# Norms ahead of the K phase, a later weight load and an earlier first gate/up block in a two-layer attention and gated-MLP kernel

## The chip, the cores and the metric

The kernel runs on one core of a Trainium2 chip. The metric is the device time of one execution in microseconds (us). Executions of the kernel before agree within 0.4%. "Faster" or "slower" needs 2%. A profile also shows TensorE's granted clock, as a share of full speed; in every profile here it is either 1.0 or 0.5 ("half clock"), and a mean between them is a mixture.

## The reference, cut to what matters

```python
x = A_x                                          # 2048 tokens x 576, bf16
x = x + A(layernorm(x), wqkv, w_phi, wo)         # attention
x = x + B(layernorm(x), w_gate, w_up, w_down)    # (x@w_gate * x@w_up) @ w_down, 4608 wide
x = x + A(layernorm(x), wqkv, w_phi, wo)         # the same again: "layer 2"
x = x + B(layernorm(x), w_gate, w_up, w_down)

def A(x, wqkv, w_phi, wo):      # linear attention, 32 heads of 18
    q, k, v = heads(x @ wqkv)
    phi_q = concat(softmax(q @ w_phi), softmax(-(q @ w_phi)))    # per head
    phi_k = concat(softmax(k @ w_phi), softmax(-(k @ w_phi)))
    kv, z = phi_k^T @ v, sum_s phi_k             # over ALL tokens
    return (phi_q @ kv) / (phi_q @ z + 1e-6) @ wo
```

The sum over all tokens is a barrier: no attention output exists before the last K tile is done. The MLP (gate, up, down) has none.

## The kernel before

The tokens form 16 tiles of 128 and 8 blocks of two tiles (a pair). Python "threads" describe the work (a pair's layer norm, a tile's K softmax, a tile's attention output, a block of gate/up, its down), and a list scheduler puts their instructions into one fixed order per engine before anything runs. At each step it takes the request that could start first; the priority decides between equals and who gets a shared buffer first, and some priorities have a head start, the "bias", in ns:

```python
key = (est - self.bias.get(int(th.prio), 0.0), -th.prio)      # smallest key is issued next
self.NPS, self.NSM, self.NVX, self.NET, ... = 2, 4, 2, 3, ... # buffers shared by the threads
self.qlead, self.pace, self.bias = 3, (4, 3), {10: 300.0}
```

So the order that runs on the chip is the one that the scheduler's own durations gave.

```python
def t_layer1(self):                          # K phase of layer 1, cut
    for b in range(NB):
        yield ("wait", ("ld", "x", b))
        yield ("go", s.t_ln(b, ("xT", 1, b)), 6, ...)              # norm of a pair, DMA transposes
        if b >= 1:
            yield ("wait", ("xT", 1, b - 1))
            for j in range(2):
                yield ("go", s.t_ain(1, 2 * b - 2 + j), 6 + ..., ...)   # K softmax, V, K^T V
    yield ("go", s.t_barrier(1), 9, "bar1")  # masks K^T V into BD
    yield ("go", s.t_q(1), 5, "q1")          # starts the outputs, pair after pair:
#   for b in range(NB):
#       if b >= s.pace[L - 1]: wait for the down of block b - pace
#       for j in range(2): yield ("go", s.t_aout(L, 2 * b + j), 7 + ..., ...)

def pol1(b):                                 # what block b of gate/up waits for besides its own norm
    if b + 1 < NB:
        ev += [("x1", 1, 2 * b + 2), ("x1", 1, 2 * b + 3)]         # outputs of the NEXT pair
```

A tile's output thread (`t_aout`) first makes the "front" (Q projection and softmax, transposes), which doesn't need BD, then waits for BD and makes the rest. `x1` is a tile's state after the attention output has been added.

Of the kernel before, what the change touches and what calls it, by code (L numbers as in the profile page):

```python
# [229 lines left out]
class _Thread:  # L230
    __slots__ = ("gen", "prio", "req", "name", "deps_cache", "est", "t_ready", "seq")
# [14 lines left out]
class Sched:  # L246

    def __init__(self, tracker):
        self.tr = tracker
        self.free_at = {e: 0.0 for e in ENGINES}  # L250
        self.busy = {e: 0.0 for e in ENGINES}
        self.threads = []
        self.pools = {}
        self.events = set()
        self.ev_time = {}
        self.dma_free = {e: 0.0 for e in ENGINES}
        self.dma_bw = 280.0
        self.dma_lat = 2000.0
        self.log = []
        self.bias = {}  # L260
        self.pe_mode = 0
        self.pe_switch = 100.0
        self.lock = None

# [56 lines left out]
    def run(self):  # L321
        tr = self.tr
        while True:
            progressed = False
            again = True
            while again:
                again = False
                for th in list(self.threads):
                    while th.req is not None and th.req[0] not in ("ops", "dma", "acq", "acqn"):
# [26 lines left out]
                        elif kind == "unlock":  # L356
                            assert self.lock is th
                            self.lock = None
                            self._advance(th, None)
                        elif kind == "delay":  # L360
# [22 lines left out]
            for th in self.threads:  # L383
                r = th.req
                if r[0] == "ops":
# [20 lines left out]
            r = th.req  # L406
# [46 lines left out]
T0 = [0, TW, 2 * TW, 3 * TW, D - TW]  # L453
# [22 lines left out]

class K:
    def __init__(self, nc, A_x, A_wqkv, A_w_phi, A_wo, B_w_gate, B_w_up, B_w_down, out):
# [3 lines left out]
        self.NPS, self.NSM, self.NVX, self.NET, self.NXP, self.NWD, self.NG, self.NO = 2, 4, 2, 3, 2, 4, 2, 1  # L482
        self.early = 2
        self.qlead = 3
        self.pace = (4, 3)
        self.bias = {10: 300.0}
# [4 lines left out]
    def alloc(self):  # L491
# [8 lines left out]
        self.kvacc = A("kvacc", [TW, NJ, TW + 1], F32)  # L500
# [31 lines left out]
        self.den = A("den", [128, self.NO, NT * HT], F32)  # L532
# [34 lines left out]
    def t_init(self):  # L567
# [30 lines left out]
            Op(100, lambda e: e.memset(s.vx[:, :, :, TW:TW + 1], 1.0), writes=[("vxone",)]),  # L598
# [10 lines left out]
    def t_bdphi(self):  # L609
        s = self  # L610
        yield ("wait", "init")
        yield ("wait", ("ld", "wphi"))
        wb = s.wst[:].unsqueeze(2).to_broadcast([TW, NT, HT, DH])
        mb = s.mask[:].rearrange("p (j d) -> p j d", j=HT).unsqueeze(1).to_broadcast([TW, NT, HT, DH])
        ov = s.BDphi[:].rearrange("p t (j d) -> p t j d", j=HT)
        yield ("ops", "dve", [Op(750, (lambda e: e.tensor_tensor(ov, wb, mb, ALU.mult)),
                                 reads=[("wst",), ("mask",)], writes=[("BDphi",)])])
        yield ("sig", "bdphi")

    def t_load(self):  # L620
# [15 lines left out]
        def rawload(which, kt):  # L636
# [7 lines left out]
                 ((lambda e: e.dma_start(s.wst[:, 4, :], s.A_w_phi[H - HT:H].rearrange("j d f -> (j d) f"))), [("wst",)], TW * DH * 2)]  # L644
# [28 lines left out]
        for i, (emit, writes, nbytes) in enumerate(items):  # L673
            if i % 3 == 0 and 5 + i // 3 < NB:
                yield ("wait", ("xT", 1, 5 + i // 3))
# [4 lines left out]
    def t_fuse(self, which):  # L680
# [7 lines left out]
        for kt in range(5):  # L688
# [6 lines left out]
            for t in range(NT):  # L695
                c0 = off + T0[t]
                ops.append(Op(60, (lambda e, t=t, c0=c0, P=P, kt=kt: e.transpose(P[0:TW, 128 * t:128 * t + 128], s.Wraw[:, kt, c0:c0 + TW], s.ident[:])),
                              reads=[("Wraw", 0, which, kt), ("Wraw", 1), ("ident",)], writes=[("pbd", bank)], excl=[("pb", bank)]))
            yield ("ops", "pe", ops)
            yield ("ops", "act", [Op(700, (lambda e, P=P, wt=wt: e.copy(s.WT[:, wt, :, :], P[0:TW, 0:640].rearrange("p (t n) -> p t n", t=NT))),  # L700
                                     reads=[("pbd", bank)], writes=[("WT", wt)], excl=[("pb", bank)])])
# [3 lines left out]
    def t_fuse2(self, which):  # L705
        s = self
        Wm, km = (s.Wq, "Wq") if which == "q" else (s.Wk, "Wk")
        for kt in range(5):
            yield ("wait", ("wt", which, kt))
            wt = s.wt_of[(which, kt)]  # L710
            for half in range(2):
# [3 lines left out]
                for t in ((0, 1, 2) if half == 0 else (3, 4)):  # L715
                    lo = 0 if t < 4 else 3 * DH
                    n = TW - lo
                    ops.append(Op(d_pe(n) + 25, (lambda e, t=t, c=c, lo=lo, n=n, bank=bank, wt=wt: e.matmul(
                        s.ps[:, bank, c:c + n], s.WT[:, wt, t, :], s.BDphi[:, t, lo:TW], start=True, stop=True)),
# [5 lines left out]
                yield ("ops", "dve", [Op(d_dve(c), (lambda e, bank=bank, c0=c0, c=c, kt=kt, m=m: e.tensor_copy(  # L725
                    Wm[0:m, kt, c0:c0 + c], s.ps[0:m, bank, 0:c])),
                    reads=[("pbd", bank)], writes=[(km,)], excl=[("pb", bank)])])
# [6 lines left out]
    def t_ln(self, b, sig):  # L734
        s = self
        x_sb, xln, st, mv, lnv, rstd, xT = s.x_sb, s.xln, s.st, s.mv, s.lnv, s.rstd, s.xT
        pair = yield ("acq", "xlnp")
        sl = [2 * pair, 2 * pair + 1]
        ss = [2 * b, 2 * b + 1]
        ops = []  # L740
        for j in range(2):
# [5 lines left out]
        for j in range(2):  # L747
# [3 lines left out]
        var2 = mv[:, sl[0]:sl[0] + 2, 1:2].rearrange("p a b -> p (a b)")  # L751
        mean2 = mv[:, sl[0]:sl[0] + 2, 0:1].rearrange("p a b -> p (a b)")
        nm = s.nmean
        yield ("ops", "act", [
            Op(215, (lambda e: e.activation(lnv[:, sl[0]:sl[0] + 2], var2, ACTF.Ln, bias=s.epst[:, 0:1], scale=1.0)),
               reads=[("mv", sl[0]), ("mv", sl[1]), ("epst",)], writes=[("lnv", pair)]),
            Op(160, (lambda e: e.mul(nm[:, sl[0]:sl[0] + 2], mean2, -1.0)),
               reads=[("mv", sl[0]), ("mv", sl[1])], writes=[("nmean", pair)]),
            Op(205, (lambda e: e.activation(rstd[:, sl[0]:sl[0] + 2], lnv[:, sl[0]:sl[0] + 2], ACTF.Exp, scale=-0.5)),  # L759
               reads=[("lnv", pair)], writes=[("rstd", pair)]),  # L760
        ])
        ops = []
        for j in range(2):
            ops.append(Op(800, (lambda e, j=j: e.tensor_scalar(  # L764
                xln[:, sl[j], 0:576], x_sb[:, ss[j], :], nm[:, sl[j]:sl[j] + 1], rstd[:, sl[j]:sl[j] + 1],
                ALU.add, ALU.mult)),
                reads=[("x", ss[j], 0), ("x", ss[j], 1), ("nmean", pair), ("rstd", pair)], writes=[("xln", sl[j])]))
        yield ("ops", "pool", ops)
        yield ("ops", "act", [Op(240, (lambda e: e.copy(xln[:, sl[0]:sl[0] + 2, 576:640], xln[:, sl[0]:sl[0] + 2, 512:576])),
                                 reads=[("xln", sl[0]), ("xln", sl[1])], writes=[("xlnt", pair)])])  # L770
        for j in range(2):
            tok = slice(128 * ss[j], 128 * ss[j] + 128)
            yield ("dma", s.g_xt[sl[j]], (lambda e, j=j, tok=tok: e.dma_start_transpose(xT[:, :, tok], xln[:, sl[j], :])),
                   [("xln", sl[j]), ("xlnt", pair)], [("xT", ss[j])], 128 * 640 * 2, False, True, 1250.0)
        yield ("rel", "xlnp", pair)
        yield ("sig", sig)
# [14 lines left out]
    def softmax_front(self, st_, pz, sm, Wm, km):  # L791
        s = self
        psb, dd, mxmn, ss = s.psb, s.dd, s.mxmn, s.ss
        gots = yield ("acqn", ["pb"], 2)
# [7 lines left out]
        ops = [Op(680, (lambda e: e.tensor_reduce(mxmn[:, pz, 0, :], p3, AX.X, ALU.max)),  # L802
                  reads=[("psb", pz, 0), ("psb", pz, 1)], writes=[("mx", pz)])]
        for h in range(2):
# [7 lines left out]
        yield ("ops", "pool", [Op(1170, (lambda e: e.tensor_tensor(d1, p3, mxb, ALU.subtract)),  # L812
                                  reads=[("psb", pz, 0), ("psb", pz, 1), ("mx", pz)], writes=[("dd", sm, 0)])])
# [31 lines left out]
        for br in range(2):  # L845
            ev = dd[:, sm, br, :].rearrange("p (g e) -> p g e", e=DH)
            rb = ss[:, sm, H * br:H * br + H].unsqueeze(2).to_broadcast([128, H, DH])
            yield ("ops", "pool", [Op(1150, (lambda e, ev=ev, rb=rb: e.tensor_tensor(ev, ev, rb, ALU.mult)),  # L848
                                      reads=s.ddk(sm, br) + [("ss", sm)], writes=s.ddk(sm, br))])

    def t_v(self, L, st_):
# [4 lines left out]
        for h in range(2):  # L856
            (_, bank), = yield ("acqn", ["pb"], 1)
            c0, n = ((0, 3 * TW), (3 * TW, D - 3 * TW))[h]
            yield ("ops", "pe", s.proj(st_, c0, n, s.Wv, "Wv", bank))
            if h == 0:  # L860
                src = s.ps[:, bank, 0:n].rearrange("p (t n) -> p t n", t=3)
                dst = s.vx[:, vxs, 0:3, 0:TW]
# [459 lines left out]
```

## Time and profile before

| | before |
|---|---|
| time, median (lowest to highest of 3 runs) | 1218.46 us (1218.12 to 1219.91) |
| span of the profiled execution | 1212.5 us |
| BD of layer 1 done by VectorE (two clearing memsets of GpSimd follow, until 114.1) | 112.6 us |
| first gate/up matmul, layer 1 / layer 2 | 140.70 / 720.58 us |
| weight load of layer 1's last down matmul ends | 667.63 us |

I cut the span at these events into four stages: prologue, main part of layer 1 (gate/up to the last down), transition, main part of layer 2. The columns are the stretch, its length, then busy time and number of instructions of PE (TensorE's matmuls), PEld (its weight loads), DVE (VectorE), ACT (ScalarE) and POOL (GpSimd), the granted clock, the DMA share and GB/s. Length less PE's busy time is TensorE's idle time.

```profile
0.00:140.70 140.70, 98.64 (x780) 70.59 (x781) 106.15 (x242) 84.11 (x220) 87.00 (x93) 0.85 0.50 142
140.70:667.63 526.93, 519.42 (x7259) 400.77 (x7301) 266.21 (x535) 193.59 (x429) 114.28 (x109) 1.00 0.34 90
667.63:720.58 52.95, 30.19 (x239) 22.17 (x237) 33.97 (x88) 22.46 (x52) 21.83 (x22) 0.81 0.11 27
720.58:1212.50 491.92, 475.73 (x6821) 363.44 (x6856) 191.31 (x380) 142.50 (x276) 50.23 (x48) 1.00 0.35 95
```

TensorE idles 42.1 us of the prologue and 22.8 of the transition. In the main parts PE has fewer records than PEld (42 and 35 fewer), so matmul records are missing and the idle time there, 7.5 and 16.2 us, is too high by several us; I use idle time only for prologue and transition. Two more stretches: two blocks of layer 2, one with a pair of outputs in it and one without.

```profile
8.00:105.00 97.00, 72.34 (x571) 50.07 (x569) 78.92 (x166) 62.59 (x173) 67.26 (x65) 0.88 0.65 187
```

```profile
783.66:846.56 62.90, 61.48 (x880) 47.43 (x886) 27.48 (x57) 20.45 (x40) 8.49 (x8) 1.00 0.32 92
1096.28:1152.37 56.09, 54.58 (x791) 40.40 (x796) 13.99 (x23) 10.85 (x19) 0.00 (x0) 1.00 0.42 110
```

A pair is 90 weight loads (886 less 796) and 6.8 us, 76 ns a load.

### The profile page before, as it was taken

The page shows a single profiled execution, that of the slowest core. Times are in us where ns is not written, and L with a number is a line of the kernel's source. Part 1 is how long each engine was busy: PE and PEld are TensorE (multiplying, and loading weights), DVE is VectorE, ACT ScalarE, POOL GpSimd, SP SyncE. Part 2 cuts the span into 40 slices and gives each one's busy share as a digit, 9 for nine tenths or more (in the row PEclk, how much of TensorE's full clock was granted, in tenths as well). Part 3 has the DMA queues.
Part 4 walks back from the last instruction along what each step waited for, and adds up shares of the span by engine and source line. Part 5 has one row for each costly group of instructions (what it writes and reads, how often), then busy time and mean ns, then how long its engine had stood idle before and what let it go on. Part 6 is the DMA issues. An engine that isn't in the chain of part 4 may idle for free.

```text
span 1212.5 us, 33465 instructions
## 1 busy us (share of the span) xinstructions
PE 1124.0 (93%) x15096; PEld 857.0 (71%) x15172; DVE 597.6 (49%) x1243; ACT 442.7 (37%) x976; POOL 273.3 (23%) x271
## 2 busy tenths in 40 slices
PE   5875899999999999999999579899999999999998
PEld 4554686868777786858585358586868686868584
DVE  7866846373645546343435483235353535353131
ACT  5765543352524334323234353123332323242120
POOL 4785403041322304020203341002020202020000
PEclk8986999999999999999999799999999999999999
DMA  7654007143341506050515100606151424343514
GB/s 175 140 161 170 17 8 183 29 123 78 89 111 51 150 13 173 18 176 13 173 18 147 41 12 13 197 3 171 28 157 43 138 62 128 72 119 81 150 39 147
DMA packets 130336, 115.59 MB, mean 95 GB/s; under 512 B 48914, under 2 KB 129042, under 8 KB 129042
## 3 DMA queue, kind: packets, MB, share of 16 engines
q1 hardware_dynamic: 130194, 113.46, 34.8%
q8 instruction: 118, 1.93, 0.7%
q14 instruction: 24, 0.20, 0.1%
HBM read 100.59 MB, written 2.36 MB: 85 GB/s over the span
## 4 chain that ended last, share of the span: by engine, by line
PE 78%; DMA 10%; DVE 5%; POOL 3%; ACT 2%; issue 1%; SPq 0%; DVEq 0%; POOLq 0%
PE ps L1079 47%; PE ps L1146 12%; PE ps L787 11%; DMA wdr<-in_B_w_down_dram 9%; PE ps L1149 3%; POOL dd L848 2%; PE ps L973 1%; DVE ss L834 1%; PE ps L990 1%; PE ps L876 1%; DVE o L1015 1%; DMA xT<-xln 1%; PE ps L1026 1%; POOL xln L764 1%; DVE mxmn L807 1%
## 5 line engine op out<-in xcount | busy, mean ns | idle before, releaser
L1079 PE MATMUL ps<-xT,Wg 64*128 64x256 bf16 x4608 | 568.7, 269 | 1.7 <-DMA xT<-xln 1.7
L1079 PE MATMUL ps<-xT,Wu 64*128 64x256 bf16 x4608 | 568.6, 269 | 0.0
L1079 PEld LDWEIGHTS ps<-xT,Wg 64*128 64x128 bf16 x4608 | 431.9, 94 | 32.5 <-issue 3.3
L1079 PEld LDWEIGHTS ps<-xT,Wu 64*128 64x128 bf16 x4608 | 431.9, 94 | 27.3
L1124 DVE TENSOR_TENSOR hT<-ps,gsb 128x512 bf16<-128x512 f32 x288 | 199.1, 691 | 349.6 <-ACT gsb L1122 349.4
L1122 ACT CAST gsb<-ps 128x512 bf16<-128x512 f32 x288 | 168.7, 586 | 453.6 <-PE ps L1079 453.3
L1146 PE MATMUL ps<-wdr,hT 128*128 128x512 bf16 x1076 | 293.8, 380 | 12.2 <-DMA wdr<-in_B_w_down_dram 11.3
L1149 PE MATMUL ps<-wdr,hT 128*128 128x64 bf16 x1152 | 221.9, 193 | 6.3 <-DMA wdr<-in_B_w_down_dram 2.1
L1146 PEld LDWEIGHTS ps<-wdr,hT 128*128 128x128 bf16 x1152 | 112.6, 98 | 145.5 <-DMA wdr<-in_B_w_down_dram 31.7
L812 POOL TENSOR_TENSOR dd<-psb,mxmn 128x576 bf16<-128x576 bf16 x64 | 74.4, 1167 | 510.4 <-DVE mxmn L802 510.4
L848 POOL TENSOR_TENSOR dd<-dd,ss 128x576 bf16<-128x576 bf16 x128 | 145.6, 1165 | 104.9 <-ACT ss L842 104.9
L1079 PE MATMUL ps<-xT,Wr 64*128 64x256 bf16 x1152 | 156.9, 269 | 0.0
L1149 PEld LDWEIGHTS ps<-wdr,hT 128*128 128x128 bf16 x1152 | 112.9, 98 | 1.5
L764 POOL TENSOR_SCALAR xln<-x_sb,nmean,rstd 128x576 bf16<-128x576 bf16 x64 | 52.1, 826 | 203.6 <-ACT rstd L759 203.6
L834 DVE TENSOR_REDUCE ss<-dd 128x64 f32<-128x1152 bf16 x64 | 84.7, 1344 | 17.5 <-ACT dd L829 17.2
L1167 DVE TENSOR_TENSOR x_sb<-ps,x_sb 128x512 bf16<-128x512 f32 x32 | 21.9, 686 | 101.9 <-PE ps L1149 101.9
L802 DVE TENSOR_REDUCE mxmn<-psb 128x32 f32<-128x576 bf16 x64 | 47.7, 745 | 46.9 <-ACT psb L799 46.9
L799 ACT CAST psb<-ps 128x288 bf16<-128x288 f32 x128 | 50.3, 397 | 43.9 <-PE ps L787 41.5
L1079 PEld LDWEIGHTS ps<-xT,Wr 64*128 64x128 bf16 x1152 | 56.1, 94 | 6.8
L827 ACT ACTIVATE dd<-dd 128x576 bf16<-128x576 bf16 x64 | 43.4, 678 | 43.8 <-DVE dd L820 43.6
L787 PE MATMUL ps<-Wk,xT 128*128 128x288 bf16 x320 | 50.8, 299 | 8.7 <-DMA xT<-xln 7.1
L787 PE MATMUL ps<-Wv,xT 128*128 128x378 bf16 (+1 forms) x320 | 54.3, 305 | 2.6 <-ACT vx L866 1.7
(67 smaller groups left out, 917.8 us busy)
## 6 DMA issues: line engine op xcount, KB each, us to landing
wdr<-in_B_w_down_dram SPq DMA_DIRECT2D x288, 288.0 KB, 3.3
Wg<-in_B_w_gate_dram SPq DMA_DIRECT2D x4, 1152.0 KB, 9.3
Wu<-in_B_w_up_dram SPq DMA_DIRECT2D x4, 1152.0 KB, 9.2
x_sb<-in_A_x_dram SPq DMA_DIRECT2D x8, 288.0 KB, 3.2
out_dram<-x_sb SPq DMA_DIRECT2D x8, 288.0 KB, 2.7
Wraw<-in_A_wqkv_dram SPq DMA_DIRECT2D x8, 144.0 KB, 2.9
xT<-xln SPq DMA_TRANSPOSE x64, 3.2
Wv<-in_A_wqkv_dram SPq DMA_DIRECT2D x1, 576.0 KB, 4.5
```

The lines of the kernel that those rows point to most:

```text
L764: ops.append(Op(800, (lambda e, j=j: e.tensor_scalar(xln[:, sl[j], 0:576], x_sb[:, ss[j], :], nm[:, sl[j]:sl[j] + 1], rstd[:, sl[j]:sl[j] ...
L787: ops.append(Op(d_pe(n), (lambda e, lhsT=lhsT, rhs=rhs, k=k: e.matmul(s.ps[:, bank, 0:n], lhsT, rhs, start=(k == 0), stop=(k == 4))), read ...
L799: yield ("ops", "act", [Op(d_actc(288), (lambda e, h=h, bank=bank: e.copy(psb[:, pz, 288 * h:288 * h + 288], s.ps[:, bank, 0:288])), reads ...
L802: ops = [Op(680, (lambda e: e.tensor_reduce(mxmn[:, pz, 0, :], p3, AX.X, ALU.max)), reads=[("psb", pz, 0), ("psb", pz, 1)], writes=[("mx", ...
L812: yield ("ops", "pool", [Op(1170, (lambda e: e.tensor_tensor(d1, p3, mxb, ALU.subtract)), reads=[("psb", pz, 0), ("psb", pz, 1), ("mx", pz ...
L834: Op(1320, (lambda e: e.tensor_reduce(ss[:, sm, :].rearrange("p (b g) -> p b g", b=2), e4, AX.X, ALU.add)), reads=s.ddk(sm, 0) + s.ddk(sm, ...
L848: yield ("ops", "pool", [Op(1150, (lambda e, ev=ev, rb=rb: e.tensor_tensor(ev, ev, rb, ALU.mult)), reads=s.ddk(sm, br) + [("ss", sm)], wri ...
L1079: out.append(Op(54.3, (lambda e, bank=bank, cs=cs, lhsT=lhsT, rhs=rhs, st=st, sp=sp: e.matmul(ps[:, bank, cs], lhsT, rhs, start=st, stop=s ...
L1122: yield ("ops", "act", [Op(540, (lambda e, g=g, gb=gb: e.copy(gsb[:, g, :], ps[:, gb, :])), reads=[("gu", gb)], writes=[("gsb", g)], excl= ...
L1124: yield ("ops", "dve", [Op(625, (lambda e, g=g, ub=ub, p=p: e.tensor_tensor(hT[:, p, :], ps[:, ub, :], gsb[:, g, :], ALU.mult)), reads=[(" ...
L1146: ops.append(Op(d_pe(512), (lambda e, lhsT=lhsT, bank=bank, slot=slot, fi=fi, f=f: e.matmul(ps[:, bank, 0:512], lhsT, s.wdr[:, slot, fi, 0 ...
L1149: ops.append(Op(d_pe(64) + 3, (lambda e, lhsT=lhsT, sl=sl, slot=slot, fi=fi, f=f: e.matmul(ps[:, Z, 64 * sl:64 * sl + 64], lhsT, s.wdr[:, ...
```

## The change

Its intent: keep VectorE fed in the K phase (norms ahead), keep the weight load out of the way, start gate/up as soon as tiles 0 and 1 are out, and treat the last K tiles of layer 2 and the first output tiles of each layer as urgent (priority 11, TensorE transposes instead of a transposing DMA). In the last two K tiles of both layers VectorE becomes an alternative to GpSimd. The title under which the change was handed in also named minima and second subtraction taken from PSUM; these stand in the kernel before already. The diff, cut to its core:

```diff
-        self.NPS, self.NSM, self.NVX, self.NET, ... = 2, 4, 2, 3, ...
+        self.NPS, self.NSM, self.NVX, self.NET, ... = 3, 4, 2, 4, ...
-        self.qlead = 3
-        self.pace = (4, 3)
-        self.bias = {10: 300.0}
+        self.qlead = 4
+        self.alt = 1.2
+        self.lnlead = 9
+        self.pol0 = 1
+        self.pace = (5, 4)
+        self.bias = {10: 300.0, 11: 800.0}
 # weights of gate and up
-            if i % 3 == 0 and 5 + i // 3 < NB:
-                yield ("wait", ("xT", 1, 5 + i // 3))
+            yield ("wait", ("xT", 1, NB - 1) if i > 1 else ("xT", 1, 6))
 # softmax of K: GpSimd or VectorE, whichever would end first, in the last two tiles
+            yield ("alt", [(eng, [Op(dur, ... e.tensor_tensor(ev, ev, rb, ALU.mult) ...)])
+                           for eng, dur in (("pool", 1150), ("dve", 675))[:1 + (crit > 1)]])
-        yield from s.softmax_front(st_, ps_, sm, s.Wk, "Wk")
+        sm = yield from s.softmax_front(st_, ps_, s.Wk, "Wk", 2 if st_ >= NS - 2 else 1 if L == 1 else 0)
 # outputs
         yield ("wait", ("BD", L))
+        if st_ < 2:
+            yield ("prio", 11 + (NS - st_) / 100.0)
-                yield ("go", s.t_aout(L, 2 * b + j), 7 + (NS - 2 * b - j) / 100.0, ...)
+                yield ("go", s.t_aout(L, 2 * b + j), (4 if b == 0 else 7) + (NS - 2 * b - j) / 100.0, ...)
 # norms of layer 1
-            yield ("go", s.t_ln(b, ("xT", 1, b)), 6, "lnA1_%d" % b)
+                if 2 * b >= s.lnlead:
+                    yield ("wait", ("ain", 1, 2 * b - s.lnlead))
+                yield ("go", s.t_ln([2 * b, 2 * b + 1], [("xT", 1, b)], False), 7, "lnA1_%d" % b)
 # what a block waits for
-            if b + 1 < NB:
+            if b >= s.pol0 and b + 1 < NB:
                 ev += [("x1", 1, 2 * b + 2), ("x1", 1, 2 * b + 3)]
```

Cut away: head groups of 7, 7, 7, 7, 4 instead of five overlapping sevens, V in 504 and 72 columns instead of 378 and 198, the norm of one tile alone with five TensorE transposes ("fast"), and the split of BD's masking between VectorE and GpSimd in layer 2.

## The prediction

> **What bounds the kernel now.** I began with the busy shares and the slices of the page.
>
> ```profile
> PE 1124.0 (93%) x15096; PEld 857.0 (71%) x15172; DVE 597.6 (49%) x1243; ACT 442.7 (37%) x976; POOL 273.3 (23%) x271
> ...
> PE   5875899999999999999999579899999999999998
> ...
> PEclk8986999999999999999999799999999999999999
> ```
>
> TensorE is the bound of most of the span. It is short of work in two places: the first five slices (the first layer's K phase, its barrier, the first output tiles) and slices 23 to 25 (the same between the layers). Next I cut the span at the events of the timeline and asked for busy time per stretch (columns: PE, PEld, DVE, ACT, POOL with counts, granted clock, DMA share, GB/s).
>
> ```profile
> 8.00:40.00 32.00, 22.57 (x172) 15.87 (x171) 27.52 (x68) 19.29 (x55) 18.42 (x20) 0.84 0.58 144
> ...
> 62.00:80.00 18.00, 16.01 (x143) 11.41 (x142) 17.41 (x32) 14.44 (x38) 17.13 (x16) 1.00 0.55 207
> 80.00:91.00 11.00, 7.30 (x44) 4.61 (x43) 1.51 (x3) 4.10 (x12) 6.29 (x7) 0.71 0.41 104
> 91.00:113.00 22.00, 11.42 (x79) 8.06 (x78) 15.74 (x30) 11.45 (x28) 12.89 (x12) 0.66 0.59 232
> 113.00:141.00 28.00, 20.93 (x176) 15.85 (x176) 20.48 (x58) 13.67 (x30) 11.92 (x13) 0.84 0.06 12
> 141.00:667.00 526.00, 518.49 (x7250) 399.99 (x7287) 265.91 (x535) 193.45 (x428) 113.65 (x108) 1.00 0.34 90
> 667.00:676.00 9.00, 1.75 (x21) 1.24 (x19) 3.24 (x10) 2.91 (x7) 4.29 (x5) 0.76 0.42 115
> 676.00:697.00 21.00, 13.39 (x78) 9.45 (x79) 10.53 (x21) 7.54 (x19) 7.31 (x8) 0.70 0.04 9
> 697.00:721.00 24.00, 16.09 (x157) 12.38 (x157) 20.61 (x58) 12.22 (x28) 10.86 (x10) 0.93 0.07 14
> ```
>
> From 62 to 80 us the K phase is bound by VectorE (17.4 of 18 us). From 80 to 91 VectorE does 1.5 us of work in 11: a hole. From 141 to 667, and again after 721, TensorE is 98% busy; only its amount of work counts there. The timeline shows the hole:
>
> ```profile
> 79.89 0.27 DVE L748 BATCH_NORM_AGGREGATE mv<-st 128x2 f32<-128x12 f32 x2
> ...
> 82.42 1.62 POOL L764 TENSOR_SCALAR xln<-x_sb,nmean,rstd 128x576 bf16<-128x576 bf16 x2
> ...
> 84.41 2.53 SPq L773 DMA_TRANSPOSE xT<-xln  x2
> ...
> 91.66 0.75 DVE L802 TENSOR_REDUCE mxmn<-psb 128x32 f32<-128x576 bf16 x1 [9.01 <-ACT psb L799]
> ```
>
> The last pair's layer norm is ended only when the earlier tiles are done, so VectorE waits 9 us for normalize, transposing DMA, projection and copy. The K/V barrier (matrix BD) then ends at 112.6, the first gate/up matmul is at 140.7. In the second layer BD ends at 696.7 and gate/up begins at 720.58.
>
> **What the Trainium skill says.** "VectorE: DVE Perf Modes", section "The three transpose paths": a 128x128 transpose takes 390 ns on TensorE and 1309 ns by DMA, and TensorE's lands in PSUM. The trace agrees in direction: the DMA that transposes one 128x640 tile takes 2.6/3.2/5.3 us (least, median, most) to landing; five TensorE transposes take 0.45 us warm and the copy 0.69. "TensorE: Matmul & The Clock Gate", Part 1: the clock is halved when idle and full after about 3.4 us of activity. The stretches at 0.66 to 0.76 against 1.00 in the dense ones agree. "SBUF — State Buffer", section "Who interferes with whom": VectorE and GpSimd share a port pair when VectorE reads two SBUF inputs or is in a two-port mode. The GpSimd multiplies here took 1160 to 1172 ns whatever ran beside them, so there is no sign of it before; the few operations that the change may move to VectorE could meet it. "DMA: Bandwidth & Descriptors", section "Where 436 GB/s comes from", has a ceiling of 435 GB/s; the gate/up load reached 437 here in its best slices.
>
> **Part 1: norms ahead, weights later.** The title's last part (minima and second subtraction from PSUM) is in the kernel before already and the diff leaves it, so it is worth 0. Layer norms now start as their x lands, up to nine tiles ahead. VectorE's K-phase work stays: the sums over exponentials start at 67.01, 70.64, 74.26, so a tile without its norm costs 3.63 us; a pair's norm costs 1.53+0.27 = 1.80. From 9 us on: 16 x 3.63 = 58.1, seven pairs x 1.80 = 12.6, casts of fused Wk 4.0, and of Wq's 4.5 about half, as ScalarE may take the rest: 77 us. With 2 us idle at the start, 3 from the last sum to the last K/V matmul, 2 for BD and 4 for imperfect packing, BD ends at 97 instead of 112.6: **15 us earlier**. The softmax fronts of tiles 0 and 1 (7.3 us of VectorE) have low priority and must be done by about then as well. GpSimd needs 16 x (0.83 + 3 x 1.165) = 69 us, below VectorE. The weights, 9.4 MB after the last transpose (I expect some 50 us), need at the 400 GB/s seen between 91 and 103 us some 24 us: in by 80, not on the path.
>
> **Part 2: from BD to gate/up.** Before, block 0 waited for tiles 0 to 3; now (pol0 = 1) for tiles 0 and 1, whose priority rises after the barrier. In layer 2 tile 0 went from 697.29 (first output matmul) to 706.6 (second residual add), with about 2.3 us of VectorE detours for other tiles in between: 7 without them. Tile 1 follows some 3.5 behind. Its own norm: statistics 0.92, ScalarE 0.70, normalize 0.35 to 0.83, tail copy 0.30, transposes 0.45, copy 0.69, semaphores 0.5: 4. Sum 14.5 against 28.1 (layer 1) and 23.9 (layer 2). Layer 1's gate/up so starts at 97+14.5 = 111.5, **29 us earlier**.
>
> **Part 3: between the layers.** Down ends at 667.7, first K projection at 676.22. One tile at a time, with TensorE transposes, it starts at about 672.5: 3.7 saved. From there to BD before: 20.5. The last two tiles may use VectorE for a multiply (0.675 by the change's own figure against 1.165), and BD's masking may be split with GpSimd: 15.5, so 5 saved. With 9.4 of part 2 gate/up starts some **18 to 19 us earlier**.
>
> **What comes back.** Tiles 2 and 3 still need TensorE. Their work goes from stretches where it filled holes into dense block 0. A block with one pair of outputs took 62.90 us (783.66 to 846.56), one without 56.09 (1096.28 to 1152.37): 6.8 us a pair, 13.6 for both layers. The heads are now split 7,7,7,7,4 instead of overlapping in the last tile; that drops the clearing memsets of BD (4 x 0.2 us on GpSimd) and some columns, but at some 57 ns per small matmul weight loads set the pace, so little time. V goes from 378+198 to 504+72 columns: five matmuls of 72 at 57 ns instead of 198 at 85 save 0.14 us, the others cost 0.28 more: +0.1 us a tile, 1.6 us in the dense part. PSUM evacuations split into two instructions cost ScalarE some 0.1 us each; it is 37% busy.
>
> Sum: 29 + 19 - 13.6 - 1.6 = 33 us; 1218.5 - 33 = 1185.5, so **1186 us**.
>
> **Rivals.** (a) The new slack is not used: VectorE, 95% busy in the K phase, is the real bound, and norms done early only delay the tiles. Then only the hole's end is saved. For it: all engines wait on VectorE there. Against it: the hole at 80 to 91 is 9 us of true idleness, and windows up to 40 us have 4.5 us more. BD would end at 103 and the time be about 1192. (b) The weight load becomes the new wait: issued in one burst after the last transpose. If pair 7's norm slips to 75 us, the load ends at 100 to 105 and still before 111; it binds only if the rate halves. The time would be about 1195. (c) Block 0 chokes on tiles 2 to 5: policy needs pair 2 before block 1, so block 0 carries two pairs beside its own evacuations on ScalarE and VectorE; a stall of 5 to 8 us in each layer gives 1198. Against it: block 140.7 to 208.6 already carried about two pairs at 67.10 of 67.90 us busy. (d) TensorE stays warm and the author's tuning packs better than I do: BD at 92, layer transition 23 us shorter, 1175.
>
> **Range and chances.** The two starts are each uncertain by some 6 us, the returned work by 4; together some 12 us each way, wider upward for (a) to (c): 1170 to 1203. Two per cent is 1194, 8 us above my centre: faster by over 2% at 0.72, within 2% at 0.27, slower by over 2% at 0.01.
>
> **What would show each step.** Norms early: no idle of several us before the max reduction of the last K tiles, BD at 93 to 101. Weights: landed before 85 us. First gate/up matmul at 106 to 117, with five TensorE transposes ahead of it rather than a transposing DMA. From the last down block to gate/up of layer 2: 53 us before, 34 to 36 after. Given back: block 0 of each layer longer by about one pair, 62.5 to 69 us or more; dense blocks else the same within 1 us. I am wrong if gate/up starts as predicted but the blocks grow by more than 14 us in sum, or if VectorE still has holes in the K phase.

## More of the kernel before

The spans of the profiles are up to 8 us off the median of the timed runs, so I take times from the timed runs and places from the profiles. In the K phase up to 105 us VectorE is busy 78.92 of 97 us.

## The result, and the profile after

The changed kernel took 1218.97 us (median of 4 runs, 1218.15 to 1220.31), the kernel before in the same rounds 1218.29 us (1216.61 to 1219.91). The ratio is 1.0007, 95% interval 0.9989 to 1.0024: **the same**, not 1186. A ratio here is always the mean time of one kernel's runs over that of the other's of the same rounds, so it isn't quite the ratio of the medians.

From the page of the changed kernel, PE's busy share and the slices of PE and of its clock:

```profile
PE 1130.3 (93%) x15202; PEld 846.2 (70%) x15202; DVE 603.6 (50%) x1277; ACT 458.8 (38%) x1077; POOL 264.4 (22%) x258
...
PE   5775799999999999999999589999999999999997
...
PEclk8997899999999999999999889999999999999999
```

The second dip is two slices instead of three; the first is still there. The same four stages of the changed kernel:

```profile
0.00:141.70 141.70, 95.64 (x800) 65.54 (x800) 107.54 (x243) 88.55 (x254) 79.75 (x84) 0.89 0.46 138
141.70:675.35 533.65, 522.82 (x7286) 395.32 (x7286) 267.24 (x547) 197.83 (x453) 115.89 (x110) 1.00 0.34 89
675.35:714.44 39.09, 22.50 (x179) 15.14 (x175) 26.96 (x66) 18.00 (x51) 10.63 (x11) 0.81 0.07 22
714.44:1217.00 502.56, 489.32 (x6941) 370.22 (x6941) 201.89 (x422) 154.43 (x322) 58.16 (x55) 0.99 0.34 93
```

| stage | before | after | difference | predicted |
|---|---|---|---|---|
| prologue | 140.7 | 141.7 | +1.0 | -29 |
| main part, layer 1 | 526.9 | 533.7 | +6.7 | some +8 |
| transition | 52.9 | 39.1 | -13.9 | -18.5 |
| main part, layer 2 | 491.9 | 502.6 | +10.6 | some +7 |
| span | 1212.5 | 1217.0 | +4.5 | -33 |

The prologue didn't get shorter at all, and what the transition gave, the two main parts took back. That layer 1's +6.7 lies near its forecast is luck: the +8 stood for a pair that an early start moves into block 0, and layer 1 had no early start. Block 0 took 78.2 us instead of 67.8 because the new pace let one more pair into it (1028 weight loads instead of 953), and block 4, which had held that pair, took 61.3 instead of 68.1.

The prologue holds a puzzle. The norms do run ahead: the last transposing DMA is at 66.00 us instead of 84.41, the hole of 80 to 91 us is filled, the weights load at 425 GB/s meanwhile, and BD is done at 104.8 us instead of 112.6. Timeline, stretch of the old hole, and the K phase to 105 us:

```profile
66.00 2.52 SPq L822 DMA_TRANSPOSE xT<-xln  x2
```

```profile
80.00:91.00 11.00, 8.52 (x78) 5.61 (x76) 8.51 (x14) 7.40 (x18) 7.71 (x7) 1.00 1.01 425
8.00:105.00 97.00, 69.30 (x591) 45.70 (x590) 80.34 (x168) 64.52 (x191) 66.68 (x62) 0.93 0.61 188
```

VectorE is busy 8.51 us where it was busy 1.51. But over the whole K phase to 105 us it is busy 80.34 instead of 78.92: its idle time, 18.1 us before and 16.7 now, was spread out rather than used. Nearly all of it is three waits: for TensorE's part of the fused Wq, for ScalarE's exponentials, and for the copy of a projection (columns: us in total, times, longest):

```profile
DVE Wq L762 <- PE ps L754: 5.9, 4, 3.1
DVE ss L886 <- ACT dd L881: 5.7, 4, 2.5
DVE mxmn L853 <- ACT psb L850: 4.4, 2, 3.8
```

Before, the sums over exponentials came one by one, 3.63 us apart (67.01, 70.64, 74.26). Now the tiles go in twos, 9.2 us for two or 4.6 a tile, with a wait for the exponentials each time:

```profile
72.74 2.61 DVE L886 TENSOR_REDUCE ss<-dd 128x64 f32<-128x1152 bf16 x2 [2.48 <-ACT dd L881]
...
81.90 2.61 DVE L886 TENSOR_REDUCE ss<-dd 128x64 f32<-128x1152 bf16 x2 [2.32 <-ACT dd L881]
```

And from BD to gate/up the kernel now takes 36.9 us instead of 28.1. The first matmul that reads BD begins at 113.99 us, against 116.89 before, so 2.9 us is all that the earlier BD gave. The timeline of VectorE after BD shows the order in which the tiles' own norms begin (the statistics are x2 for a tile alone, x4 for a pair):

```profile
121.86 0.82 DVE L782 BATCH_NORM_STATS2 st<-x_sb 128x6 f32<-128x288 bf16 x2
...
135.15 1.53 DVE L782 BATCH_NORM_STATS2 st<-x_sb 128x6 f32<-128x288 bf16 x4
...
137.67 0.82 DVE L782 BATCH_NORM_STATS2 st<-x_sb 128x6 f32<-128x288 bf16 x2
```

Tile 0 is first, then comes the pair of tiles 2 and 3, and tile 1, which block 0 waits for, is the last of the four. Then TensorE starts gate/up and stands again, because its next PSUM bank is still read by the second subtraction (L872) of another tile's Q front:

```profile
145.31 0.28 PE L1136 MATMUL ps<-xT,Wg 64*128 64x256 bf16 x1 [2.35 <-DVE dd L872]
```

After this stall gate/up ran at half clock from 146.9 to 150.4 us.

### The profile page after: what moved, and what is told of

The parts are those of the page before. It is cut to its first block, busy times and chain, and to the rows that moved or that the text cites. A ratio compares the mean times of both kernels' runs of the same rounds, so it can differ in the third digit from the quotient of the medians. Undisturbed runs are those within 1.5% of the kernel's fastest.

```text
span 1217.0 us, 33727 instructions
## 1 busy us (share of the span) xinstructions
PE 1130.3 (93%) x15202; PEld 846.2 (70%) x15202; DVE 603.6 (50%) x1277; ACT 458.8 (38%) x1077; POOL 264.4 (22%) x258
## 4 chain that ended last, share of the span: by engine, by line
PE 78%; DMA 9%; DVE 6%; ACT 4%; POOL 2%; issue 1%; SPq 0%; DVEq 0%
PE ps L1136 47%; PE ps L1203 14%; PE ps L837 10%; DMA wdr<-in_B_w_down_dram 9%; PE ps L1206 2%; PE ps L1026 1%; PE ps L1047 1%; DVE ss L886 1%; PE ps L931 1%; POOL dd L900 1%; DVE mxmn L853 1%; DVE mxmn L858 1%; PE ps L1083 1%; DVE dd L872 1%; ACT dd L879 1%
## 5 line engine op out<-in xcount | busy, mean ns | idle before, releaser
L1203 PE MATMUL ps<-wdr,hT 128*128 128x512 bf16 x1152 | 311.5, 381 | 14.3 <-DMA wdr<-in_B_w_down_dram 13.6
L863 POOL TENSOR_TENSOR dd<-psb,mxmn 128x576 bf16<-128x576 bf16 x61 | 71.0, 1167 | 493.6 <-DVE mxmn L853 493.5
L1136 PE MATMUL ps<-xT,Wr 64*128 64x256 bf16 x1152 | 163.2, 270 | 0.0
L804 POOL TENSOR_SCALAR xln<-x_sb,nmean,rstd 128x576 bf16<-128x576 bf16 x58 | 47.2, 826 | 182.8 <-ACT rstd L800 182.8
L1136 PEld LDWEIGHTS ps<-xT,Wr 64*128 64x128 bf16 x1152 | 61.4, 94 | 7.0
L1029 ACT COPY eT<-ps 126x512 bf16<-126x512 bf16 (+1 forms) x128 | 52.6, 423 | 23.2 <-PE ps L1026 21.1
L837 PE MATMUL ps<-Wv,xT 128*128 128x504 bf16 (+1 forms) x320 | 52.6, 298 | 4.1 <-ACT vx L920 3.4
```

What stands on the lines that cost most here:

```text
L837: ops.append(Op(d_pe(n), (lambda e, lhsT=lhsT, rhs=rhs, k=k: e.matmul(s.ps[:, bank, 0:n], lhsT, rhs, start=(k == 0), stop=(k == 4))), read ...
L863: yield ("alt", [(eng, [Op(dur, (lambda e: e.tensor_tensor(d1, p3, mxb, ALU.subtract)), reads=[("psb", pz, 0), ("psb", pz, 1), ("mx", pz)] ...
L1029: yield ("ops", "act", [Op(dur, (lambda e, et=et, P=P, r=r, t0=t0, t1=t1: e.copy(s.eT[0:r, et, t0:t1, :], P[0:r, 128 * t0:128 * t1].rearra ...
L1136: out.append(Op(54.3, (lambda e, bank=bank, cs=cs, lhsT=lhsT, rhs=rhs, st=st, sp=sp: e.matmul(ps[:, bank, cs], lhsT, rhs, start=st, stop=s ...
L1203: ops.append(Op(d_pe(512), (lambda e, lhsT=lhsT, bank=bank, slot=slot, fi=fi, f=f: e.matmul(ps[:, bank, 0:512], lhsT, s.wdr[:, slot, fi, 0 ...
```

## The experiments

Four theories. **T1, order**: pair 0's priority 4 makes tiles 0 and 1 late, so the early start isn't there in layer 1. **T2, moved work**: an early start moves TensorE's work into block 0; only the idle time that vanishes is gained. **T3, clock**: gate/up of layer 2 starts at half clock. **T4, ports**: VectorE and GpSimd hinder each other where VectorE takes multiplies over. An edit also changes the order that the scheduler finds, so I read the stages and not the total alone. A single profile's places vary too: in six profiles whose K phase has the changed kernel's instructions in the changed kernel's order, BD comes between 104.7 and 110.9 us. The latest two had 20.5 us of half clock before 105 us, the others 8 to 13. Each group of runs shares one chip and the runs of the kernel before; all ran with 5 rounds and gave correct results.

### First rounds: order, early start, alternatives

Raise tiles 0 and 1 as soon as BD is there:

```diff
         yield ("sig", ("BD", L))
+        for th in s.sc.threads:
+            if th.name in ("aout%d_0" % L, "aout%d_1" % L):
+                th.prio = 11 + (NS - int(th.name[-1])) / 100.0
```

> Edit: when the K/V barrier of a layer is done, the output threads of tiles 0 and 1 are raised at once to the priority that they would else take only at their next step. T1 (order: in layer 1 tile 1, which gate/up waits for, is overtaken by tiles 2 and 3 because pair 0 has priority 4 until it has passed the wait; tile 1's second residual add is at 137.6 us, after those of tiles 2 and 3): tiles 0 and 1 are first again, the first gate/up matmul comes at 126 to 131 us instead of 141.7, and the time falls by nearly as much, to about 1207 us. T2 (TensorE has the same work; what starts earlier comes back in block 0): gate/up also starts 11 to 15 us earlier, but layer 1's blocks grow by one pair's 6.8 us and more, because tiles 2 and 3 now stand in block 0; the time falls by 2 to 6 us only. If the first gate/up matmul stays within 3 us of 141.7, both are wrong.

Ratio to the kernel before 1.0004 (0.9988 to 1.0021). Tiles 0 and 1 are out at 125.5 and 129.8 us, before tiles 2 and 3. Gate/up starts at 133.5 us, somewhat later than either theory said, as BD itself came at 110.9 in this profile; BD to gate/up took 22.6 us instead of 36.9. The main part of layer 1 grew to 543.9 us, 10.3 more than the changed kernel's. The start is 8.2 us earlier. The ratio is the changed kernel's own of its first rounds (1.0007) and 0.5% under that of the third rounds (1.0054), so somewhere between nothing and 6 us of it arrives.

Give pair 0 the common priority:

```diff
-  yield ("go", s.t_aout(L, 2 * b + j), (4 if b == 0 else 7) + (NS - 2 * b - j) / 100.0, ...)
+  yield ("go", s.t_aout(L, 2 * b + j), 7 + (NS - 2 * b - j) / 100.0, ...)
```

> Edit: pair 0's output threads get the base priority 7 that all other pairs have, instead of 4. Their softmax fronts then run inside the K phase. T1: barrier some 4 to 5 us later than 104.8 us (the fronts of tiles 0 and 1 take VectorE's time there), but gate/up starts at 124 to 130 us, because nothing is left but the outputs; time 1205 to 1209 us. T2: the same start, time 1212 to 1216 us. In layer 2 nothing should change by more than 2 us, since there tiles 0 and 1 are first in both.

Ratio 0.9992 (0.9974 to 1.0010), 1213.92 us beside 1214.42. Gate/up starts at 125.9 us, 15.8 us before the changed kernel's: the order was the reason that layer 1 started late. But BD is done at 111.8 us, 7.0 later. In another profile of this very kernel, from the last rounds, it is 109.3, with as much half clock before 105 us as the changed kernel had (12.5 and 12.7 us): 4.5 later. So more than half of the 7.8 us by which BD had come earlier was the fronts of tiles 0 and 1, pushed from before BD to behind it. The main part of layer 1 takes 546.3 us, 12.7 more than the changed kernel's. T1 is right about the start and, as far as rounds without the changed kernel can tell, wrong about its worth.

Start late again in both layers:

```diff
-        self.pol0 = 1
+        self.pol0 = 0
```

> Edit: block 0 of each layer waits for tiles 2 and 3 again (pol0 = 0), all else as in the changed kernel. In layer 1 tile 1 is last anyway, so the start at 141.7 us should not move by more than 1 us and the early start has been worth nothing there (T1 and T2 agree). In layer 2 gate/up starts 15 to 19 us later, at 730 to 734 us. If an early start is worth its full size less the 6.8 us of one pair, the time grows by 8 to 12 us, to 1227 to 1231 us; if it all comes back (T2 at its strongest), by less than 3 us. T3 (the cold TensorE clock at the early start costs some 3 us): here gate/up of layer 2 starts at a granted clock of 1.0.

Ratio 1.0102 (1.0082 to 1.0123). Layer 1's gate/up at 142.6 us, less than 1 us moved: the early start was inert there, as both expected. In layer 2 it is at 734.5 us, 20 us later, with the clock at 1.00, and the main part is 13.9 us shorter. The early start of layer 2 is worth something, but much less than 20 us.

Keep the last K tiles on GpSimd:

```diff
-  sm = yield from s.softmax_front(st_, ps_, s.Wk, "Wk", 2 if st_ >= NS - 2 else 1 if L == 1 else 0)
+  sm = yield from s.softmax_front(st_, ps_, s.Wk, "Wk", 1 if L == 1 else 0)
```

> Edit: the subtraction and the multiplies of the last two K tiles of each layer stay on GpSimd, as in the kernel before. T4 (VectorE and GpSimd hinder each other on SBUF: VectorE's multiply took 1.6 us beside GpSimd instead of 0.75 alone, so the alternatives gain nothing): barriers of both layers at the same place within 1.5 us, time the same within 2 us. Against T4 (the alternatives are worth what the change expects of them): both barriers 2 to 5 us later, time 3 to 6 us longer.

Ratio 1.0097 (1.0081 to 1.0113), 0.4 to 0.9% above the changed kernel's two ratios from other rounds. BD of layer 1 comes at 108.4 us (+3.6, at 11.5 us of half clock), but gate/up still starts at 141.6. From the first K projection of layer 2 to its BD it is 22.1 us instead of 20.9; other runs with the alternatives have up to 21.8. So T4's "gain nothing" falls for layer 1's BD; the expected 2 to 5 us in layer 2 did not show, and where the longer time comes from stays open. The hindrance itself is real. Three of VectorE's operations of this form in the timeline of the changed kernel, and the GpSimd operation that began with the third:

```profile
92.54 1.62 DVE L900 TENSOR_TENSOR dd<-dd,ss 128x576 bf16<-128x576 bf16 x1
95.47 1.44 DVE L863 TENSOR_TENSOR dd<-psb,mxmn 128x576 bf16<-128x576 bf16 x1
100.97 0.75 DVE L900 TENSOR_TENSOR dd<-dd,ss 128x576 bf16<-128x576 bf16 x1
```

```profile
100.98 1.76 POOL L900 TENSOR_TENSOR dd<-dd,ss 128x576 bf16<-128x576 bf16 x1 [1.43 <-ACT ss L894]
```

The first two began while GpSimd was in a run of such multiplies and took 1.62 and 1.44 us. The third began 0.01 us before GpSimd's: it took 0.75 us, and GpSimd's took 1.76 instead of the 1.16 to 1.17 of the kernel before. In these operations whoever came second waited. Layer 2 shows it once more: VectorE's multiply from 696.34 us took 0.76, GpSimd's from 696.38 took 1.74.

### Second rounds: one part undone at a time

Layer 1's start late again, with the order mended:

```diff
 # on top of pair 0 at priority 7, in layer 1 only
-            if b >= s.pol0 and b + 1 < NB:
+            if b + 1 < NB:
```

> Edit: as the run in which pair 0 has priority 7 (its gate/up of layer 1 began at 125.9 us in the profile, 15.8 us before the changed kernel's, and its time was only about 1 us better), but block 0 of layer 1 waits for tiles 2 and 3 again; layer 2 stays as changed. It asks what an early start of layer 1 is worth by itself. T2 (only TensorE's idle time counts; the work of tiles 2 and 3 moves into block 0): gate/up at 146 to 150 us, blocks 0 and 1 together 15 to 20 us shorter than with the early start, the end 3 to 7 us later, 1217 to 1221 us. T1 (the early start is worth its size less 6.8 us): the end 13 to 16 us later.

Ratio 1.0039 (1.0025 to 1.0052). Gate/up at 150.8 us, 24.9 later; blocks 0 and 1 together take 142.5 us instead of 160.1, 17.6 shorter; the span is 3.6 longer. That is T2's expectation, but for a start 0.8 us later than it said. The comparison of times crosses rounds, so the last rounds below repeat it properly.

The launch of the norms as it was:

```diff
-                if 2 * b >= s.lnlead:
-                    yield ("wait", ("ain", 1, 2 * b - s.lnlead))
-                yield ("go", s.t_ln([2 * b, 2 * b + 1], [("xT", 1, b)], False), 7, "lnA1_%d" % b)
+            yield ("go", s.t_ln([2 * b, 2 * b + 1], [("xT", 1, b)], False), 6, "lnA1_%d" % b)
 # and the K tiles of a pair launched in the same loop, as shown in the kernel before
```

> Edit: the launch of the layer norms of layer 1 is the one of the kernel before (each pair's norm when its x has landed, at priority 6, K tiles of a pair launched after the pair before is transposed); everything else as changed. My prediction's part 1 gave the norms' lead 15 us, of which 8 showed (barrier at 104.8 instead of 112.6). If the lead itself did this, the barrier goes back to about 112 us and VectorE idles again for several us before the last K tiles; time 4 to 8 us longer. If the lead is worth nothing and the 8 us came from the rest (the last two K tiles taking VectorE for their multiplies, which without it came at 108.4, and the weight load), the barrier stays within 1.5 us of 104.8 and the time within 2 us of the changed kernel's.

Ratio 1.0015 (1.0001 to 1.0029), BD at 106.7 us (+1.9, with 10.2 us of half clock before 105). The hole at 80 to 91 us does not come back (VectorE busy 8.52 us in it), so another part of the change closed it; which one, no run shows. The lead is worth some 2 us of BD and no time that shows. In the changed kernel the last pair is transposed some 16 us before the maximum of its first tile is taken; that slack is not used.

The weights as they were:

```diff
-            yield ("wait", ("xT", 1, NB - 1) if i > 1 else ("xT", 1, 6))
+            if i % 3 == 0 and 5 + i // 3 < NB:
+                yield ("wait", ("xT", 1, 5 + i // 3))
```

> Edit: the gate/up weights are issued three by three behind the transposes of pairs 5 to 7, as in the kernel before; everything else as changed. If the weight load's transfers held up the transposing DMAs of the last pairs (a second reading of the hole at 80 to 91 us), the hole comes back, the barrier ends 3 to 8 us later and the time is longer by 2 to 6 us. If not, barrier and time stay within 1.5 us: the later issue was worth nothing.

BD at 104.7 us, gate/up at 141.7: not moved by 0.2 us. The span is 1213.6 us, but the timed ratio is 1.0048 (1.0029 to 1.0067) with runs from 1215 to 1224 us. Since the changed kernel's own ratio moves as far between chips (below), I call its time inconclusive; the later issue bought nothing at the barrier.

Eight unread matmuls while tile 1's norm of layer 2 runs:

```diff
+        if warm:     # only the norm of tile 1, layer 2
+            (_, wbank), = yield ("acqn", ["pb"], 1)
+            yield ("ops", "pe", [Op(220, ... e.matmul(s.ps[:, wbank, 0:512], s.ident[:], s.Wg[:, 0, 0:512], ...)) for _ in range(8)])
```

> Edit: while tile 1's norm of layer 2 is under way, TensorE gets eight matmuls of 512 columns whose result nobody reads, in the bank that the tile's transposes then overwrite. T3 (gate/up of layer 2 starts with the clock at half, from 714 to 720 us, which costs about 3 us): the clock in the first 6 us of block 0 is 1.0 instead of 0.5, the start is at most 1 us later, and the time falls by 2 to 3 us. Against T3: the clock stays at 0.5, or the block's length doesn't change, and the time is the same or 1 to 2 us longer.

Ratio 1.0019 (0.9998 to 1.0040). In its profile the clock is 1.00 from the start of block 0, which takes 75.9 us instead of 78.5, and the transition takes 1.0 us more. In time nothing shows.

### Third rounds: the changed kernel again, the pace, and the clock

> The changed kernel itself, unaltered, so that it stands in the same rounds as the two below: every theory expects 1.000 to 1.003 of the kernel before, layer 1's gate/up at about 141.7 us and layer 2's stretch from gate/up to the end at 500 to 503 us.

Ratio 1.0054 (1.0032 to 1.0076), 1224.07 us beside 1218.27: worse than expected, and a warning that ratios of different rounds differ by half a per cent for the same kernel. The stages are as they were (gate/up at 141.8 and 715.9 us). One thing is not. The first 6 us of gate/up in layer 2, first in the earlier profile of this kernel, then in this one (the column before the last two is the clock):

```profile
713.60:717.00 3.40, 2.62 (x28) 1.77 (x28) 3.38 (x7) 3.30 (x6) 1.17 (x1) 0.50 0.00 0
717.00:720.40 3.40, 3.40 (x36) 2.35 (x34) 1.35 (x1) 0.01 (x1) 0.00 (x0) 0.50 0.00 0
```

```profile
715.92:719.00 3.08, 3.08 (x58) 2.75 (x60) 3.02 (x6) 2.57 (x5) 1.07 (x1) 1.00 0.00 0
719.00:722.00 3.00, 3.00 (x49) 2.27 (x45) 2.82 (x5) 2.07 (x7) 1.09 (x1) 1.00 0.00 0
```

The same instructions ran at half clock in one execution (36 matmuls in 3.4 us) and at the full clock in the other (58 in 3.1). So T3's loss is not in every execution, but it goes with the early start: of the twelve profiles in which layer 2 starts early and has no unread matmuls ahead, ten have a half-clock stretch of 3.4 or 6.8 us at that start. The three with the late start and the two with unread matmuls have none.

The timed runs carry a mean clock each, and it goes with the time: the six of these rounds run from 1218.67 us at 0.978 to 1228.71 at 0.971. Their mean clock is 0.9742, that of the first rounds 0.9780. My estimate, as the clock is 0.5 or 1.0: 9 us more at half clock in 1220 us, which costs up to 4.6, nearly all of the 4.7 us between the two mean times. So a part of what differs between rounds, and between executions, is how long TensorE stood at half clock.

Pair 0 at priority 7, and the pace of the output pairs as before:

```diff
-        self.pace = (5, 4)
+        self.pace = (4, 3)
```

> Edit: pair 0 at priority 7, and the pace of the output pairs back at the kernel before's 4 and 3 blocks ahead instead of 5 and 4. With pair 0 at priority 7 alone, layer 1 from gate/up to the end of down took 546.3 us against 533.7, and TensorE was idle 16.2 us of it against 10.8; from 245 to 265 us VectorE was 91% busy and TensorE waited for tiles 8 and 9, which no block before the fourth needs. T2 with choking (part of the returned time is VectorE's crowding in blocks 0 and 1, because one pair more is let in than is needed): pair 4 moves to a later block, TensorE's idle time in layer 1 falls by 3 to 6 us, and the time is 2 to 5 us below that of the run with priority 7 alone, 0.995 to 0.998 of the kernel before. If the return is TensorE's work alone, the time stays at 0.999.

1212.33 us beside 1218.27, ratio 0.9948 (0.9934 to 0.9962), and 1.1% below the changed kernel in the same rounds: **better than both kernels**, if by little. Next to the run with priority 7 alone, block 1 of layer 1 takes 68.5 us instead of 80.6, and block 4, which now holds the pair, 69.4 instead of 61.9; TensorE's idle time in the main part of layer 1 falls by 2.4 us (expected: 3 to 6). Both differences to the other kernels stay under 2%.

With the eight matmuls besides:

> Edit: the run above with the eight unread matmuls ahead of tile 1's transposes in layer 2 besides. In the run where they stood alone the first block of layer 2 ran at the full clock and was 2.6 us shorter, with a transition 1 us longer. T3: 1 to 2 us below the run above. If the timed runs do not start with the clock at half as the profiled one did: the same within 1 us, or 1 us longer.

Ratio 0.9948 (0.9926 to 0.9970): no difference. Its profile is shorter (1204.3 us, full clock at the start of layer 2), but most of that lies elsewhere.

### Last rounds: what one early start is worth

> The best kernel so far (pair 0 at priority 7, pace 4 and 3), again, as the base of the three others of these rounds: 0.994 to 0.996 of the kernel before by every theory.

1212.17 us beside 1217.06, ratio 0.9958 (0.9941 to 0.9975). In its timeline tile 0's statistics are followed by tile 1's at once, where the changed kernel had 15.8 us between them:

```profile
120.12 0.82 DVE L782 BATCH_NORM_STATS2 st<-x_sb 128x6 f32<-128x288 bf16 x2
...
122.67 0.81 DVE L782 BATCH_NORM_STATS2 st<-x_sb 128x6 f32<-128x288 bf16 x2
```

The base with layer 1's block 0 waiting for tiles 2 and 3 (the edit of the second rounds):

> Edit: as the base, but block 0 of layer 1 waits for tiles 2 and 3. Gate/up of layer 1 starts 22 to 26 us later than the base's. My prediction's rule (the start's difference less 6.8 us for the pair that moves) makes that 15 to 19 us longer than the base. The counting of idle time (only what TensorE idles in the added stretch is lost) makes it 5 to 10 us: layer 1 from gate/up to the end of down shorter by 14 to 19 us.

Ratio 1.0041 (1.0024 to 1.0058). Prologue and main part of layer 1, the base first, then the late one:

```profile
0.00:127.10 127.10, 88.83 (x710) 59.67 (x710) 92.75 (x207) 79.42 (x230) 73.49 (x79) 0.88 0.51 154
127.10:670.91 543.81, 528.60 (x7337) 402.63 (x7376) 280.12 (x583) 206.75 (x476) 122.55 (x116) 1.00 0.33 87
```

```profile
0.00:151.09 151.09, 102.35 (x820) 70.25 (x820) 111.98 (x254) 95.54 (x268) 87.19 (x91) 0.84 0.42 130
151.09:682.23 531.14, 518.09 (x7229) 394.45 (x7266) 261.31 (x535) 191.72 (x438) 108.61 (x104) 1.00 0.34 89
```

The start differs by 24.0 us, the main part by 12.7 the other way. The time differs by 0.83% (1.0041 less 0.9958), 10.1 us. TensorE's idle time in the prologue is 38.3 and 48.7 us: 10.5 apart. The added 24 us hold 13.5 us of TensorE work (110 loads), which the early start only moves. The prediction's rule said 17.2 us. The idle time is not the whole account, though: the moved work is 3.0 us shorter in the base's main part (10.5 us; the late prologue ran 17 us more at half clock), and the base's main part idles 2.2 us more. That these two nearly cancel here is luck.

The base with layer 2's block 0 waiting:

```diff
-            return [("x1", 2, 2 * b + 2), ("x1", 2, 2 * b + 3)] if b >= s.pol0 and b + 1 < NB else []
+            return [("x1", 2, 2 * b + 2), ("x1", 2, 2 * b + 3)] if b + 1 < NB else []
```

> Edit: as the base, but block 0 of layer 2 waits for tiles 2 and 3. Gate/up of layer 2 starts 17 to 23 us later. By the prediction's rule 10 to 16 us longer than the base, by the counting of idle time 6 to 10 us.

Ratio 1.0047 (1.0030 to 1.0063). The transition, base and late:

```profile
670.91:708.66 37.75, 21.15 (x179) 14.71 (x175) 26.99 (x66) 18.08 (x51) 10.64 (x11) 0.85 0.07 22
```

```profile
673.97:733.96 59.99, 37.31 (x294) 26.36 (x290) 43.06 (x107) 33.19 (x87) 22.92 (x21) 0.77 0.05 14
```

The transition is 22.2 us longer, the main part 11.8 shorter (502.7 and 490.9 us), the time 0.89% or 10.8 us longer; the rule said 15.4. Idle time differs by 6.1 us only. The moved work (115 loads) took 16.2 us of TensorE in the late transition, where the clock was lower (0.77 against 0.85), and 12.4 in the base's main part: 3.7 us more. With 0.6 us of idle time in the main parts that is the 10.4 us by which these two stages differ. That the clock made the moved work dearer fits, but no run holds the clock fixed.

The base with the pace of 5 and 4:

> Edit: as the base, but with the changed kernel's pace of 5 and 4. If the crowding of VectorE in blocks 0 and 1 is real: 2 to 6 us longer than the base; if the difference of the earlier rounds (0.9992 there, 0.9948 for the base elsewhere) was between chips only: within 1.5 us.

Ratio 0.9979 (0.9958 to 1.0000), 2.0 us above the base's median: the intervals overlap, so the pace's worth is unclear. What it does is visible in block 1. Ten us of it, in the run of the first rounds with priority 7 and pace 5 and 4, and in the base:

```profile
255.00:265.00 10.00, 7.69 (x62) 5.02 (x65) 8.17 (x20) 3.97 (x11) 6.76 (x6) 0.83 0.28 71
```

```profile
255.00:265.00 10.00, 9.90 (x108) 6.84 (x109) 7.41 (x22) 6.66 (x17) 7.44 (x7) 1.00 0.70 194
```

With the higher pace TensorE idled 2.3 us there, waiting for VectorE on tiles 8 and 9. This crowding is real, but small.

## Why the prediction was wrong

**What bounds the kernel** was read rightly: TensorE in the main parts, two dips. The table even held the warning: from 113 to 141 us TensorE was busy 20.93 of 28 us.

**Part 1** failed in its sum. The last norm left the path, the hole went and the weights were not on the path, as predicted (they were in at about 96 us, not 80). But BD came at 104.8 us, not 97, and even that flatters: with pair 0 at priority 7 it came at 111.8, and at 109.3 with the clock as in the changed kernel, so 4 to 7 us were fronts put off. The undone lead cost 1.9 us. The sum also left out the 7.3 us of VectorE for those fronts, which part 2 needs done by then. The term that was too small is "2 us idle at the start, 3 from the last sum to the last K/V matmul, 2 for BD and 4 for imperfect packing": with 8.51 us busy in the old hole, VectorE still idled 16.7 of the 97 us up to 105, and a tile took 4.6 us where the sum has 3.63. (The clock has a share in this too: the kernel before had 23.8 us at half before 105 us, the changed one 12.7.)

**Part 2** held where its condition held. In layer 2, BD to gate/up took 13.5 us (predicted 14.5); in layer 1 with the order mended, 13.9. In the changed kernel layer 1 took 36.9. The step that failed is "tiles 0 and 1, whose priority rises after the barrier": they had priority 4 up to that wait, tiles 2 and 3 overtook tile 1, and it came last of the four.

**Part 3**: down to the first K projection fell from 8.6 to 4.7 us, 3.9 instead of the predicted 3.7. From there to BD it stayed at 20.9 (20.8 before), predicted 15.5; that is the step that failed. The masking of BD, now split, took 2.35 us where it had taken 2.15. The Trainium skill's "SBUF — State Buffer", section "Who interferes with whom", has one reason, an exclusive lock when VectorE reads two SBUF inputs beside a GpSimd instruction that reads SBUF. The trace agrees: one multiply of VectorE that began beside GpSimd's took 1.12 us instead of 0.75, and one of GpSimd that began just after VectorE's 1.74 instead of 1.16, about 1 us together. No run shows the rest.

**What comes back** failed, and would have failed with a perfect order too. "6.8 us a pair" per layer became 12.7 and 11.8 us where only the start was changed. The step that failed is its size: the moved work was taken for one pair's. More moved: 110 and 115 loads instead of 90, since parts of the next tiles' work wait too (40 transposes of softmax results instead of a pair's 20). And each cost more than the 76 ns a load of the pair measured in layer 2: PE's busy time in the main parts rose by 10.5 and 12.4 us (34 to 39 matmul records missing in each of the four), 95 and 108 ns a load. The prediction had named this sign: blocks that grow by more than 14 us in sum; it was 24.5. Besides, the third and fourth block of layer 1, which hold a pair and two K tiles, became longer. The third block, before and after, and the wait in it that is new:

```profile
276.73:344.96 68.23, 67.42 (x938) 52.47 (x946) 37.20 (x78) 26.58 (x60) 16.89 (x16) 1.00 0.33 89
```

```profile
288.56:357.97 69.41, 68.14 (x945) 51.77 (x946) 37.20 (x80) 27.57 (x64) 16.95 (x16) 1.00 0.33 88
```

```profile
330.11 0.20 PE L1206 MATMUL ps<-wdr,hT 128*128 128x64 bf16 x1 [0.77 <-DVE dd L872]
```

It is 1.2 us longer for the same 946 loads, 0.77 of it one wait of TensorE for the second subtraction. The predicted 1.6 us for both layers didn't contain it. Nor did V's split cost TensorE what it said: the matmuls of 72 columns began 32 ns apart, not 57.

**Rivals.** (a), slack that isn't used, is what the norms' lead met. (b), the weights, did not happen. (c), block 0 choking, happened with 2 to 3 us at the start of layer 1. None of them had the main thing, that an early start removes idle time and only moves the work; I had put in the moved work as a correction to a large gain, where it was more than half of it.

What stays open: why the K tiles now go in twos and VectorE is not fed better (its waits are above; no run removed one; undoing the norms' lead left the twos: 79.5 and 80.8, 89.0 and 90.2 us), and how much of each difference is the clock.

## What to carry to other kernels

When one engine bounds the time, a milestone that comes earlier is not a gain: count that engine's busy time in the stretch that disappears, and expect its idle time there, and some more where its work ran at a lower clock; here 24 us of earlier start were worth 10, and 22 were worth 11. Look at the granted clock before explaining a few us between two profiles. In a kernel whose order comes from a list scheduler, check after each change of priorities that the thing waited for really comes first: a low priority before a wait can cost more than a high one behind it gives. An earlier barrier may only mean that other work was moved behind it.

## What the Trainium skill lacked or had wrong

- "TensorE: Matmul & The Clock Gate", Part 1, has the clock fall after a whole idle window of some 3.4 us, and run-to-run variation from a free-running window. The variation agrees: the same kernel began layer 2 at 0.50 and at 1.00. But TensorE need not be idle for a whole window: before the fall it was busy 1.46 us of the 3.4 from 710.2 to 713.6 us, and its longest gap was 1.42 us. (A later part of the page tells of a clock that swings when TensorE pauses often and briefly, which fits.) What share of a window counts as idle is not stated. Counted over the full-clock windows of 3.41 us in the 17 profiles here, from the clock's own steps: each with TensorE busy for less than 0.43 of it was followed by half clock, none with more than 0.57, and between these both happened.
